# Other places in a hand written order of issue: cosformer attention and a feed-forward layer on one core

## The chip, the cores and the metric

The kernel runs on one core of a Trainium2 chip. The metric is the time of one execution on the device in microseconds (us). A core has engines that run side by side, each with its own queue of instructions in program order: TensorE (PE in the profile; matmuls from SBUF into PSUM), VectorE (DVE), ScalarE (ACT), GpSimd (POOL) and SyncE (SP, which here issues nearly all DMAs). An instruction that waits holds up everything behind it in its engine's queue.

## The reference

Linear attention with a cosine weighting, and then a feed-forward layer over all its tokens. There are 8 batches, 8 heads, 576 positions and 64 features per head; 4608 tokens of 512 features go through 512 to 2048 to 512.

```python
pos = np.arange(S); theta = np.pi / 2 * pos / S
def phi(x):                                  # 64 -> 128 features
    r = np.maximum(x, 0)
    return np.concatenate([r * cos(theta), r * sin(theta)], axis=-1)
q_p, k_p = phi(q), phi(k)
kv  = einsum('bhsf,bhsd->bhfd', k_p, v)
z   = k_p.sum(axis=2)
num = einsum('bhsf,bhfd->bhsd', q_p, kv)
den = einsum('bhsf,bhf->bhs', q_p, z) + 1e-6
x   = (num / den) as [4608, 512]
h   = x @ w_in                               # 512 -> 2048
out = maximum(0.01 * h, h) @ w_out           # 2048 -> 512
```

## The kernel before

**Groups.** The tokens are handled in nine groups. Group g from 0 to 7 holds the first 512 tokens of batch g; group 8 holds the last 64 tokens of all eight batches. A group passes these steps, named by the functions that issue them:

- `loads` (SP): q, k and v of the batch, each 1 MB in float32, into `qst`, `kst`, `vst`; small tails into `ktl`, `vtl`.
- `k_part(b, j, part, engine)` and `q_part(g, j, part, engine)`: relu and cosine (part 0, "c") or sine (part 1, "s") weight for the j-th 128 tokens, float32 to float16, on VectorE (`L240`) or ScalarE (`L238`). Results: `kpm`, `kpt` (the tail, j = 4) and `qp`. `v_part` casts v (`vmain` in two halves, `vtail`).
- `kv_all` (PE): k_p^T v of all heads into `ps_kv`, copied to `kv` on ScalarE.
- `q_transpose_dma(g, j)` (SP): a DMA transpose of `qp` into `qpT`, called qT g j below. It needs both parts of this j.
- `num(g, j)` (PE `L380`): numerator and denominator into the single PSUM buffer `ps_num`; then three VectorE steps, `den` (L391), `rden` (L395) and the product `xs` (L396).
- `x_transpose_dma(g, j)` (SP `L357`): `xs` into `xT`, called xT g j below. Batch 2 has PE transposes in its place (`x_transpose`).
- `x_sums(g, s)`, s = 1 to 4 (DVE `L254`, tiles `xw`, `x`): differences of blocks of `xT`, each needing all four xT.

**The feed-forward layer of groups 2 to 8** takes 2x2 blocks and seven products in place of eight. `p1(g, t, n, bank)` (PE `L785`) is product n = 1 to 7 of a pair t of hidden rows, four matmuls of 256 columns into one of four PSUM banks; `seed`, `lrelu`, `u_copy`, `u_lrelu` (ScalarE, L795, L798, L805, L812) and `u_add` (VectorE L251) combine and apply the leaky ReLU into tile `g`. Product 5 opens the bank JOIN, `u_add(g, t, 1)` reads it, and product 3 then adds into that bank, so product 3 waits for the read. Groups 2 and 3 do four hidden rows (6, 7, 14, 15) with plain matmuls, `f1_one` (PE L495), each followed by its own activation (L770). The second layer has `g_sums` (DVE, L251 and L254, tiles `g`, `gs`), `p2` (PE L890), `o_copy` (ScalarE L908), `o_add` (DVE L251) and `o_store` (SP). `w1_sums` and `w2_sums` are sums of the weights on VectorE.

**The order.** From group 1 on nothing is planned by a scheduler. Each step is entered with `put(position, function, arguments)`, the list is sorted by position, and the functions issue their instructions in that order, so a position is a place in the queue of every engine that the step uses. Between engines only the data dependencies order the work. The positions stand in tables:

- `F1_AT`, `F4_AT`: places of the steps behind p1 (seed, copies, adds, leaky ReLU), relative to the product; F1_AT for groups 2 and 3, F4_AT from group 4.
- `F2_AT`, `F24_AT`: of the copies, adds and stores behind p2.
- `W1_AT`, `W2_AT`, `R_AT`: of the weight sums. `G1_AT` (group 1), `G_AT` (2), `G3_AT` (3), `G4_AT` (4 to 7), `GL_AT` (8): of g_sums.
- `ENG[b]`: which engine does each cast of batch b. `AT[b]`: positions of the casts, loads, transposes, num and x_sums of batch b; entry n of `xs` is x_sums(b, n + 1). Entry 5 of both serves batches 5 to 8.

`top[g]` is the position at which group g's first product stands: 46, 104, 162, then 56 more for each group. The entries of AT[2] and AT[3] are absolute; those of AT[4] and AT[5] are relative to `top[b]`. The order is set by these lines:

```python
put(s0 + at_["qs"][j], q_part, b, j, 1, eng["qs"][j])
put(s0 + at_["qt"][j], q_transpose_dma, b, j)
put(s0 + at_["xs"][j], x_sums, b, j + 1)
...
for _, _, f, args in sorted(line, key=lambda e: e[:2]):
    f(*args)
```

Of the kernel before, what the change touches and what calls it, by code (L numbers as in the profile page):

```python
# [18 lines left out]
def kernel(  # L19
# [798 lines left out]
    F1_AT = {'seed': (0.3, 0.7, 0.5), 'u1': (1.0, 1.0, 1.0), '11': (5.3, 1.3, 2.8), 'u2': (0.3, 0.7, 0.5), '22': (1.8, 0.6, 0.2), '21': (0.5, 0.8, 1.9), '12': (0.5, 1.6, 1.1), 'out': (2.7, 2.7, 2.1)}

    P_AT = (  # L820
# [3 lines left out]
    )  # L824
# [3 lines left out]
    F4_AT = {'seed': 1.0, 'u1': 4.1, '11': 7.9, 'u2': 7.6, '22': 9.4, '21': 10.3, '12': 11.2, 'out': 12.9}

    def f1_stream(g):  # L830

        evs = [(-0.1, quarters, (g,))]
        for t in range(3 if g < ALL else 4):
            if g < ALL:
                at_, a = P_AT[t], (g + t) % 2
            else:
# [90 lines left out]
            )  # L927

    F24_AT = {'u0': 2.7, '11': -0.2, 'u1': 1.7, 'u2': -0.7, '22': 0.6, '21': 0.5, '12': 0.0, 'low': 1.9, 'top': 3.1}
    F2_AT = {'u0': 0.7, '11': -0.7, 'u1': -0.1, 'u2': -0.9, '22': -0.5, '21': -0.1, '12': 0.9, 'low': 2.5, 'top': 3.3}  # L930
# [236 lines left out]
```

## Time and profile before

| | |
|---|---|
| Time, median of 3 runs | 271.64 us (271.63 to 271.68) |
| The profiled execution's own time | 272.37 us |
| Its span in the profile | 270.6 us |
| Granted TensorE clock, mean | 1.00 |
| Instructions | 6617 |
| DMA | 57.05 MB, mean 211 GB/s |
| HBM read, written | 36.70 MB, 9.44 MB |

The profile is of one execution. Its page gives each engine's busy time, the span in 40 slices, the chain of work that ended last, and the costliest groups of instructions. The timeline has a row for each instruction or run of like instructions: start, length, engine, line, operation, output and inputs, and in brackets the idle time before it with the instruction that ended it. The length of a row holds some pipelining, so an engine often starts the next instruction before the length of the last is over; the distance of two starts is then the cost.

### The profile page before, as it was taken

The page shows a single profiled execution, that of the slowest core. Times are in us where ns is not written, and L with a number is a line of the kernel's source. Part 1 is how long each engine was busy: PE and PEld are TensorE (multiplying, and loading weights), DVE is VectorE, ACT ScalarE, POOL GpSimd, SP SyncE. Part 2 cuts the span into 40 slices and gives each one's busy share as a digit, 9 for nine tenths or more (in the row PEclk, how much of TensorE's full clock was granted, in tenths as well). Part 3 has the DMA queues.
Part 4 walks back from the last instruction along what each step waited for, and adds up shares of the span by engine and source line. Part 5 has one row for each costly group of instructions (what it writes and reads, how often), then busy time and mean ns, then how long its engine had stood idle before and what let it go on. Part 6 is the DMA issues. An engine that isn't in the chain of part 4 may idle for free.

```text
span 270.6 us, 6617 instructions
## 1 busy us (share of the span) xinstructions
PE 263.6 (97%) x2668; PEld 226.3 (84%) x2668; DVE 201.9 (75%) x446; ACT 200.6 (74%) x331; POOL 10.5 (4%) x21
## 2 busy tenths in 40 slices
PE   8989999999999999999999999999999999999994
PEld 6875455765898989889999999999999889999984
DVE  5965798797986897889779696978577757644653
ACT  6846556696878998798899789978966757776621
POOL 1057001000000000000000000000000000000000
PEclk9999999999999999999999999999999999999999
DMA  6999999979999969998999699977384312200324
GB/s 211 343 394 409 398 370 373 378 161 285 280 232 340 163 209 226 318 168 226 301 273 138 189 265 273 186 207 155 72 141 153 62 41 97 80 0 2 148 46 119
DMA packets 87150, 57.05 MB, mean 211 GB/s; under 512 B 56656, under 2 KB 82256, under 8 KB 86608
## 3 DMA queue, kind: packets, MB, share of 16 engines
q1 hardware_dynamic: 86672, 56.24, 78.9%
q8 instruction: 21, 0.34, 0.5%
q10 hardware_dynamic: 448, 0.39, 0.4%
q14 instruction: 9, 0.07, 0.1%
HBM read 36.70 MB, written 9.44 MB: 171 GB/s over the span
## 4 chain that ended last, share of the span: by engine, by line
PE 70%; DMA 4%; DVE 2%; ACT 1%; issue 0%; DVEq 0%
PE ps_o L890 31%; PE ps_h L785 27%; PE ps_h L495 3%; DMA qst<-in_q_dram 3%; PE ps_h L890 3%; PE ps_num L380 2%; PE ps_kv L289 2%; DMA xT<-xs 1%; DVE gs L254 0%; PE ps_kv L298 0%; ACT g L798 0%; PE ps_xt L445 0%; DVE xw L254 0%; DVE xs L396 0%; DVE w L254 0%
## 5 line engine op out<-in xcount | busy, mean ns | idle before, releaser
L890 PEld LDWEIGHTS <-g 128*128 128x128 f16 x648 | 62.6, 98 | 7.4 <-DVE g L251 0.3
L251 DVE TENSOR_TENSOR u<-ps_h,u 128x512 f32<-128x512 f32 x52 | 35.8, 688 | 25.5 <-PE ps_h L785 22.2
L890 PE MATMUL ps_o<-w,g 128*128 128x256 f16 x352 | 51.2, 273 | 0.0
L785 PEld LDWEIGHTS <-w 128*128 128x128 f16 x416 | 44.4, 114 | 1.3
L785 PE MATMUL ps_h<-xT,w 128*128 128x256 f16 x288 | 43.3, 273 | 0.0
L812 ACT ACTIVATE g<-u 128x1024 f16<-128x1024 f32 x26 | 27.5, 1058 | 10.9 <-DVE u L251 10.8
L785 PEld LDWEIGHTS <-wa 128*128 128x128 f16 x312 | 34.0, 113 | 1.8 <-DVE xw L254 0.6
L798 ACT ACTIVATE g<-ps_h 128x512 f16<-128x512 f32 x52 | 31.2, 602 | 5.7 <-PE ps_h L785 5.7
L805 ACT COPY u<-ps_h 128x512 f32<-128x512 f32 x52 | 30.4, 584 | 5.4 <-PE ps_h L785 5.4
L890 PE MATMUL ps_o<-wb,g 128*128 128x256 f16 x232 | 33.5, 273 | 0.0
L785 PE MATMUL ps_h<-xw,wa 128*128 128x256 f16 x208 | 31.3, 273 | 0.3 <-DVE xw L254 0.3
L890 PEld LDWEIGHTS <-gs 128*128 128x128 f16 x256 | 24.9, 98 | 3.0
L908 ACT COPY ob<-ps_o 128x512 f32<-128x512 f32 (+1 forms) x32 | 17.9, 561 | 10.0 <-PE ps_o L890 8.5
L495 PE MATMUL ps_h<-xT,w 128*128 128x512 f16 (+1 forms) x104 | 24.7, 363 | 0.0
L396 DVE TENSOR_TENSOR xs<-ps_num,rden 128x512 f16<-128x512 f32 x28 | 19.4, 692 | 1.0
L890 PE MATMUL ps_o<-w,gs 128*128 128x256 f16 x120 | 17.8, 273 | 0.0
L251 DVE TENSOR_TENSOR ob<-ps_o,ob 128x512 f32<-128x512 f32 (+1 forms) x22 | 14.9, 675 | 3.7 <-ACT ob L908 1.4
L890 PE MATMUL ps_o<-wb,gs 128*128 128x256 f16 x120 | 17.5, 273 | 0.0
L254 DVE TENSOR_TENSOR gs<-g 128x1024 f16<-128x1024 f16 x16 | 11.0, 689 | 8.3 <-ACT g L812 8.1
L795 ACT COPY ps_h<-ps_h 128x512 f32<-128x512 f32 x26 | 14.9, 572 | 2.2 <-PE ps_h L785 1.4
L785 PE MATMUL ps_h<-xT,wa 128*128 128x256 f16 x104 | 15.6, 273 | 0.0
L785 PE MATMUL ps_h<-xw,w 128*128 128x256 f16 x104 | 15.6, 273 | 0.0
(113 smaller groups left out, 408.9 us busy)
## 6 DMA issues: line engine op xcount, KB each, us to landing
qst<-in_q_dram SPq DMA_DIRECT2D x7, 1024.0 KB, 7.1
out_dram<-ob SPq DMA_DIRECT2D x14, 512.0 KB, 2.9
kst<-in_k_dram SPq DMA_DIRECT2D x6, 1024.0 KB, 8.3
vst<-in_v_dram SPq DMA_DIRECT2D x6, 1024.0 KB, 7.6
w1st<-in_moe_w_in_dram SPq DMA_DIRECT2D x8, 512.0 KB, 9.8
w2st<-in_moe_w_out_dram SPq DMA_DIRECT2D x4, 1024.0 KB, 12.3
kst<-in_k_dram SPq DMA_DIRECT2D x4, 512.0 KB, 7.1
vst<-in_v_dram SPq DMA_DIRECT2D x4, 512.0 KB, 7.0
```

Source lines behind the costliest of these rows:

```text
L251: nc.vector.tensor_tensor(out=o, in0=a, in1=b, op=ALU.add)
L254: nc.vector.tensor_tensor(out=o, in0=a, in1=b, op=ALU.subtract)
L289: nc.tensor.matmul(ps[:, n * NE : (n + 1) * NE - 1], lhsT=kpm[:, h, j, :], rhs=vmain[:, h, j, 0 : NE - 1], start=(n == 0 and j == 0), stop ...
L396: nc.vector.tensor_tensor(out=xs, in0=ps[:, :, 0 : 4 * NE].rearrange("p a (b e) -> p a b e", e=NE)[:, :, :, 0:D], in1=rden.rearrange("p (a ...
L495: nc.tensor.matmul(ps[:, lo:hi], lhsT=w1[m // 4][c // 2][:, c % 2, m % 4 : 512 : 4], rhs=st["xT", g][:, c, lo:hi], start=(c == 0 and lo == 0),
L785: nc.tensor.matmul(bank[:, p], lhsT=w(c), rhs=st["xb", g][n][:, c], start=(fresh and p == 0 and c == 0), stop=(c == 1), skip_group_check=True,
L795: nc.scalar.copy(bank1[bj], bank1[bi])
L798: nc.scalar.activation(st["g" + nm, g][:, 2 * t : 2 * t + 2], bank1[bi], AF.Lrelu)
L805: nc.scalar.copy(st["u", g, t][:, n], bank1[bi])
L812: nc.scalar.activation(st["gt", g][:, :, 1, 2 * t : 2 * t + 2], st["u", g, t], AF.Lrelu)
L890: nc.tensor.matmul(bank[..., lo:hi], lhsT=st[G2[n], g][:, m, pair * P : (pair + 1) * P], rhs=W2[n](m)[:, lo:hi], start=(fresh and m == 0), ...
L908: nc.scalar.copy(o_at(g, half_, col, pair), bank_of(bi, pair, pair is None))
```

## The change

Only the tables of positions and the table of engines change. No operation, buffer or data type does, and `P_AT` is only written on one line. Of the casts, these change engine: in batch 2, k parts kc[1] (to ScalarE), ks[0] and ks[3] (to VectorE); in batch 3, several; in batch 4, v's tail (to VectorE), qs[2] (to ScalarE) and qs[3] (to VectorE); in batches 5 to 8, kc[3] and qc[3] (to ScalarE), qs[0] and qs[3] (to VectorE). Everything else moves by between a tenth of a position and some twenty within its queue. The tables with their lines:

```diff
-    F1_AT = {'seed': (0.3, 0.7, 0.5), 'u1': (1.0, 1.0, 1.0), '11': (5.3, 1.3, 2.8), 'u2': (0.3, 0.7, 0.5), '22': (1.8, 0.6, 0.2), '21': (0.5, 0.8, 1.9), '12': (0.5, 1.6, 1.1), 'out': (2.7, 2.7, 2.1)}
+    F1_AT = {'seed': (0.3, 0.8, 1.3), 'u1': (1.0, 0.6, 1.0), '11': (5.7, 1.4, 2.8), 'u2': (0.3, 0.7, 0.5), '22': (1.4, 0.6, 0.2), '21': (0.5, 1.0, 2.1), '12': (0.5, 1.6, 0.5), 'out': (2.7, 2.7, 2.1)}
-    F4_AT = {'seed': 1.0, 'u1': 4.1, '11': 7.9, 'u2': 7.6, '22': 9.4, '21': 10.3, '12': 11.2, 'out': 12.9}
+    F4_AT = {'seed': 1.1, 'u1': 3.7, '11': 7.9, 'u2': 7.6, '22': 9.3, '21': 9.1, '12': 11.1, 'out': 12.9}
-    F2_AT = {'u0': 0.7, '11': -0.7, 'u1': -0.1, 'u2': -0.9, '22': -0.5, '21': -0.1, '12': 0.9, 'low': 2.5, 'top': 3.3}
+    F2_AT = {'u0': 1.5, '11': -0.5, 'u1': 0.0, 'u2': -0.9, '22': -0.2, '21': -0.1, '12': 0.5, 'low': 2.7, 'top': 3.3}
-    W1_AT = {3: (38.5, 53.5)}
-    W2_AT = {2: (16.0,), 3: (29.5, 18.5), 4: (75.5,)}
-    G1_AT = {3: (15.0, 31.0), 2: (16.5, 33.5), 1: (25.5, 39.5), 4: (63.0, 45.5)}
-    G_AT = {3: (-6.5, 10.5), 2: (0.0, 11.0), 1: (17.5, 32.5), 4: (23.0, 29.5)}
-    G3_AT = {3: (-3.5, 10.0), 2: (2.0, 23.0), 1: (12.5, 29.5), 4: (26.5, 49.0)}
-    G4_AT = {3: (-6.5, 12.5), 2: (3.0, 17.0), 1: (26.0, 18.0), 4: (33.0, 54.0)}
-    GL_AT = {3: (-15.5, 13.0), 2: (-1.5, 13.5), 1: (5.5, 16.2), 4: (17.5, 32.0)}
-    R_AT = (28.5, 30.0, 46.0, 45.0)
+    W1_AT = {3: (38.5, 51.5)}
+    W2_AT = {2: (16.0,), 3: (29.5, 18.5), 4: (70.0,)}
+    G1_AT = {3: (15.0, 32.5), 2: (26.0, 35.5), 1: (20.5, 34.0), 4: (54.0, 40.5)}
+    G_AT = {3: (-6.5, 10.0), 2: (8.5, 11.0), 1: (17.0, 31.5), 4: (24.0, 34.5)}
+    G3_AT = {3: (-4.0, 10.0), 2: (2.0, 15.0), 1: (13.5, 33.5), 4: (26.5, 54.0)}
+    G4_AT = {3: (-6.5, 13.0), 2: (0.0, 17.0), 1: (26.5, 18.0), 4: (31.0, 52.0)}
+    GL_AT = {3: (-15.5, 13.0), 2: (9.5, 14.0), 1: (3.5, 14.2), 4: (23.5, 30.5)}
+    R_AT = (20.5, 34.0, 54.0, 45.0)
...
     ENG, batch 4:
-    'v': (DVE, DVE, ACT), ... 'qs': (DVE, DVE, DVE, ACT)
+    'v': (DVE, DVE, DVE), ... 'qs': (DVE, DVE, ACT, DVE)
     AT, batch 3:
-    'num': (69.5, 76.0, 83.0, 89.0), 'xt': (89.5, 92.5, 93.0, 100.5), 'xs': (102.5, 106.0, 104.5, 114.0)
+    'num': (69.0, 76.0, 83.0, 89.0), 'xt': (92.5, 91.5, 94.5, 100.5), 'xs': (101.5, 103.5, 112.0, 114.5)
     AT, batch 4 (relative to 162):
-    'v': (-85.0, -40.5, -44.5), 'kv': (-37.5,), 'qc': (-72.5, -67.5, -58.0, -40.0), 'qs': (-66.5, -51.5, -43.5, -39.0), 'qt': (-52.0, -34.5, -33.0, -32.0)
+    'v': (-77.0, -41.0, -42.5), 'kv': (-37.5,), 'qc': (-72.5, -66.5, -53.0, -48.5), 'qs': (-66.5, -52.0, -43.5, -36.5), 'qt': (-52.5, -37.5, -38.0, -33.0)
     AT, batches 5 to 8 (relative to top; 218 for batch 5):
-    'load': (-103.5, -85.5, -75.5), 'kc': (-64.5, -75.0, -78.0, -50.0, -49.0)
-    'qc': (-87.0, -76.0, -45.0, -40.0), 'qs': (-73.5, -75.5, -44.0, -30.5), 'qt': (-55.0, -53.0, -43.5, -25.5)
-    'xt': (-24.5, -17.8, -17.6, -6.9)
+    'load': (-106.0, -87.5, -79.0), 'kc': (-65.0, -77.5, -73.0, -49.5, -54.0)
+    'qc': (-92.0, -76.5, -46.0, -40.0), 'qs': (-71.0, -75.5, -43.5, -27.5), 'qt': (-55.0, -53.0, -42.5, -25.5)
+    'xt': (-24.5, -25.8, -12.6, -7.4)
```

AT[2] (attention of batch 2) and the lines of AT not shown change in the same manner; num(2,0) and num(2,1) keep positions 19.0 and 20.5.

More of the change, by code (lines that the diff above doesn't have):

```diff
@@ L816 @@
     SEED, JOIN, ALL = 2, 3, 4
[L818 to L820 removed]
[3 rows of a table removed]
[L824 removed]
+    F1_AT = {'seed': (0.3, 0.8, 1.3), 'u1': (1.0, 0.6, 1.0), '11': (5.7, 1.4, 2.8), 'u2': (0.3, 0.7, 0.5), '22': (1.4, 0.6, 0.2), '21': (0.5, 1.0, 2.1), '12': (0.5, 1.6, 0.5), 'out': (2.7, 2.7, 2.1)}
+    P_AT = ({1: 0, 6: 3, 2: 5, 7: 6, 5: 8, 4: 9, 3: 11}, {1: 10, 6: 13, 2: 15, 7: 16, 4: 19, 5: 20, 3: 23}, {1: 21, 6: 24, 2: 26, 7: 27, 5: 28, 4: 30, 3: 31})
     ONE_AT = ((4, 7), (12, 14), (17, 18), (22, 25))
     P4_AT = {1: 0, 6: 3, 2: 5, 7: 6, 5: 8, 4: 9, 3: 11}
[L828 removed]
+    F4_AT = {'seed': 1.1, 'u1': 3.7, '11': 7.9, 'u2': 7.6, '22': 9.3, '21': 9.1, '12': 11.1, 'out': 12.9}
     def f1_stream(g):
@@ L1080 @@
-    R_AT = (28.5, 30.0, 46.0, 45.0)
-    ENG = {2: {'kc': (DVE, DVE, DVE, DVE, DVE), 'ks': (ACT, DVE, DVE, ACT, DVE), 'v': (ACT, DVE, ACT), 'qc': (DVE, DVE, DVE, DVE), 'qs': (DVE, DVE, DVE, DVE)}, 3: {'kc': (ACT, ACT, ACT, DVE, DVE), 'ks': (DVE, DVE, ACT, DVE, DVE), 'v': (DVE, ACT, DVE), 'qc': (ACT, DVE, ACT, ACT), 'qs': (DVE, DVE, DVE, ACT)}, 4: {'kc': (ACT, ACT, DVE, ACT, ACT), 'ks': (DVE, ACT, DVE, DVE, DVE), 'v': (DVE, DVE, ACT), 'qc': (DVE, ACT, ACT, DVE), 'qs': (DVE, DVE, DVE, ACT)}, 5: {'kc': (ACT, ACT, DVE, DVE, ACT), 'ks': (DVE, DVE, DVE, DVE, DVE), 'v': (DVE, ACT, ACT), 'qc': (ACT, ACT, DVE, DVE), 'qs': (ACT, ACT, DVE, ACT)}}
@@ L1082 @@
-    AT = {2: {'kc': (-12.0, -0.5, 13.0, 5.5, 13.0), 'ks': (-22.5, -12.5, -17.0, -10.5, 1.0), 'v': (8.0, 11.0, 13.0), 'kv': (16.5,), 'qc': (-8.5, 2.5, 4.5, 9.0), 'qs': (0.0, 4.5, 7.5, 13.0), 'qt': (6.0, 7.0, 8.0, 14.0), 'num': (19.0, 20.5, 24.0, 27.5), 'xt': (24.4, 24.9, 26.9, 30.9), 'xs': (36.0, 50.0, 39.0, 56.0)}, 3: {'load': (20.5, 24.0, 32.0), 'kc': (37.0, 43.0, 48.0, 52.0, 50.5), 'ks': (34.0, 43.5, 58.5, 50.5, 51.0), 'v': (56.0, 57.0, 59.5), 'kv': (62.0,), 'qc': (26.0, 29.0, 31.0, 36.5), 'qs': (31.5, 29.5, 41.0, 41.0), 'qt': (32.5, 34.5, 44.0, 48.0), 'num': (69.5, 76.0, 83.0, 89.0), 'xt': (89.5, 92.5, 93.0, 100.5), 'xs': (102.5, 106.0, 104.5, 114.0)}, 4: {'load': (-76.5, -104.5, -111.0), 'kc': (-80.0, -58.0, -56.0, -70.5, -49.5), 'ks': (-65.5, -54.5, -65.0, -54.5, -54.0), 'v': (-85.0, -40.5, -44.5), 'kv': (-37.5,), 'qc': (-72.5, -67.5, -58.0, -40.0), 'qs': (-66.5, -51.5, -43.5, -39.0), 'qt': (-52.0, -34.5, -33.0, -32.0), 'num': (-34.0, -28.3, -25.1, -16.4), 'xt': (-19.0, -16.8, -12.1, -6.4), 'xs': (-0.5, 0.0, 9.5, 17.0)}, 5: {'load': (-103.5, -85.5, -75.5), 'kc': (-64.5, -75.0, -78.0, -50.0, -49.0), 'ks': (-71.0, -59.0, -72.0, -60.5, -77.0), 'v': (-60.0, -52.0, -60.5), 'kv': (-46.5,), 'qc': (-87.0, -76.0, -45.0, -40.0), 'qs': (-73.5, -75.5, -44.0, -30.5), 'qt': (-55.0, -53.0, -43.5, -25.5), 'num': (-37.0, -32.3, -19.6, -15.9), 'xt': (-24.5, -17.8, -17.6, -6.9), 'xs': (-2.5, -1.5, -1.5, 16.0)}}
@@ new lines @@
+    ENG = {2: {'kc': (DVE, ACT, DVE, DVE, DVE), 'ks': (DVE, DVE, DVE, DVE, DVE), 'v': (ACT, DVE, ACT), 'qc': (DVE, DVE, DVE, DVE), 'qs': (DVE, DVE, DVE, DVE)}, 3: {'kc': (ACT, DVE, DVE, ACT, DVE), 'ks': (DVE, DVE, DVE, DVE, DVE), 'v': (ACT, ACT, DVE), 'qc': (ACT, DVE, ACT, ACT), 'qs': (DVE, DVE, ACT, DVE)}, 4: {'kc': (ACT, ACT, DVE, ACT, ACT), 'ks': (DVE, ACT, DVE, DVE, DVE), 'v': (DVE, DVE, DVE), 'qc': (DVE, ACT, ACT, DVE), 'qs': (DVE, DVE, ACT, DVE)}, 5: {'kc': (ACT, ACT, DVE, ACT, DVE), 'ks': (DVE, DVE, DVE, DVE, DVE), 'v': (DVE, ACT, ACT), 'qc': (ACT, ACT, DVE, ACT), 'qs': (DVE, ACT, ACT, DVE)}}
@@ new lines @@
+    AT = {2: {'kc': (-12.0, -1.5, 11.0, 5.5, 13.0), 'ks': (-25.0, -11.5, -19.0, -9.5, 1.0), 'v': (9.0, 11.0, 11.0), 'kv': (16.5,), 'qc': (-9.5, -3.5, 3.5, 9.0), 'qs': (0.0, 4.5, 6.5, 13.0), 'qt': (2.0, 7.5, 8.5, 14.5), 'num': (19.0, 20.5, 24.0, 27.5), 'xt': (24.9, 24.4, 27.9, 30.9), 'xs': (36.5, 47.0, 43.0, 59.0)}, 3: {'load': (18.5, 25.0, 31.5), 'kc': (45.0, 53.0, 47.0, 52.0, 51.5), 'ks': (46.5, 43.5, 59.5, 55.5, 48.0), 'v': (56.0, 56.5, 59.5), 'kv': (63.0,), 'qc': (28.0, 29.0, 31.0, 40.5), 'qs': (31.5, 30.0, 33.5, 41.0), 'qt': (32.5, 33.5, 49.0, 49.0), 'num': (69.0, 76.0, 83.0, 89.0), 'xt': (92.5, 91.5, 94.5, 100.5), 'xs': (101.5, 103.5, 112.0, 114.5)}, 4: {'load': (-76.5, -110.5, -112.0), 'kc': (-80.0, -59.0, -57.0, -72.5, -50.0), 'ks': (-66.0, -51.5, -65.0, -53.5, -54.0), 'v': (-77.0, -41.0, -42.5), 'kv': (-37.5,), 'qc': (-72.5, -66.5, -53.0, -48.5), 'qs': (-66.5, -52.0, -43.5, -36.5), 'qt': (-52.5, -37.5, -38.0, -33.0), 'num': (-33.5, -28.3, -25.1, -18.4), 'xt': (-21.0, -5.8, -9.6, -6.4), 'xs': (-0.5, -0.5, 9.5, 8.0)}, 5: {'load': (-106.0, -87.5, -79.0), 'kc': (-65.0, -77.5, -73.0, -49.5, -54.0), 'ks': (-71.0, -58.5, -77.0, -60.5, -77.0), 'v': (-59.5, -52.0, -61.0), 'kv': (-46.5,), 'qc': (-92.0, -76.5, -46.0, -40.0), 'qs': (-71.0, -75.5, -43.5, -27.5), 'qt': (-55.0, -53.0, -42.5, -25.5), 'num': (-37.0, -32.3, -19.6, -15.9), 'xt': (-24.5, -25.8, -12.6, -7.4), 'xs': (-2.5, -1.5, -1.5, 16.0)}}
```

3 rows, old and new, of the table P_AT are left out of this document.

## The prediction

> **What bounds the kernel now.** I read the page's busy shares and slices first, then the chain of waits.
>
> ```profile
> PE 263.6 (97%) x2668; PEld 226.3 (84%) x2668; DVE 201.9 (75%) x446; ACT 200.6 (74%) x331; POOL 10.5 (4%) x21
> PE   8989999999999999999999999999999999999994
> PE 70%; DMA 4%; DVE 2%; ACT 1%; issue 0%; DVEq 0%
> ```
>
> TensorE is the bound: 97% busy, nine tenths or more in nearly every slice, and 70% of the chain that ended last. No matmul is added or taken away, so the change can pay only through stalls of TensorE. The PE view of the waits, from the kernel's start, names few; these two fall where groups 2 and 3 are worked on:
>
> ```profile
> PE ps_num L380 <- DVE xs L396: 0.5, 1, 0.5
> PE ps_h L785 <- DVE xw L254: 0.3, 1, 0.3
> ```
>
> The timeline of PE shows both places (start, length, form).
>
> ```profile
> 60.70 0.42 PE L380 MATMUL ps_num<-kv,qpT 128*128 128x65 f16 x8
> 62.44 0.41 PE L380 MATMUL ps_num<-kv,qpT 128*128 128x65 f16 x8 [0.45 <-DVE xs L396]
> ...
> 95.87 0.60 PE L785 MATMUL ps_h<-xT,wa 128*128 128x256 f16 x4
> 96.31 0.60 PE L890 MATMUL ps_o<-w,g 128*128 128x256 f16 x4
> 97.21 0.63 PE L785 MATMUL ps_h<-xw,wa 128*128 128x256 f16 x4 [0.30 <-DVE xw L254]
> ```
>
> A product starts 0.44 us behind the last (95.87 to 96.31), as long as TensorE waits for nothing; between 96.31 and 97.21 there are 0.90, so the second stall costs 0.46. The first costs 0.6 at most: one f1_pair (two products of twice the width, 0.87) and the num (0.25) fill 1.12 of the 1.74 from 60.70. Together 1.1 us, 0.4% of the time: that is all that issue order behind this point can win. The sum below is made against the profiled execution's 272.37 us (span 270.6, 1.8 around it), 0.73 over the median of 271.64; a stall counts the same in both. About 0.2%, 0.54 us, is what a measurement of this kernel can tell from no change.
>
> **The change, part by part.** *The first stall stays.* It is num(2,0), its three DVE steps, then num(2,1) in the same PSUM buffer. Positions 19.0 and 20.5 of these two are as they were. The DVE rows:
>
> ```profile
> 61.17 0.16 DVE L391 TENSOR_SCALAR den<-ps_num 128x8 f32<-128x8 f32 x1
> 61.60 0.69 DVE L396 TENSOR_TENSOR xs<-ps_num,rden 128x512 f16<-128x512 f32 x1
> ```
>
> den starts when num's results are there (60.70 + 0.42), not when VectorE is free. The casts that change engine ahead of it (two k parts come to VectorE, one leaves, a g_sums of 0.69 goes later) alter only its slack. Nothing won: 0.
>
> *The second stall moves.* DVE rows around it:
>
> ```profile
> 94.87 0.68 DVE L251 TENSOR_TENSOR u<-ps_h,u 128x512 f32<-128x512 f32 x1
> 95.47 0.41 DVE L254 TENSOR_TENSOR xw<-xT 128x512 f16<-128x512 f16 x1
> 95.80 0.69 DVE L254 TENSOR_TENSOR gs<-g,gs 128x1024 f16<-128x1024 f16 x1
> 96.40 0.42 DVE L254 TENSOR_TENSOR x<-xT 128x512 f16<-128x512 f16 x1
> 96.74 0.42 DVE L254 TENSOR_TENSOR xw<-xT,xw 128x512 f16<-128x512 f16 x1
> 91.12 3.89 DMA xT<-xs
> ```
>
> TensorE waits at 97.21 for the last sum, x_sums(3,2), 96.74 + 0.42. Ahead of it stand a g_sums (95.80) and x_sums(3,3) (96.40), 0.60 + 0.34 of issue. After, both go behind it (g_sums 104.0 to 112.5, x_sums(3,3) 104.5 to 112.0), so this stall goes. But x_sums(3,1) goes from 102.5 to 101.5, ahead of u_add(2,2,1) at 102.4, the 94.87 row. VectorE takes its queue in order, and x_sums(3,1) cannot start before the last xT transpose has landed: 91.12 + 3.89 = 95.01. So u_add starts at 95.35 or later (95.02 + 0.33) instead of 94.87 and ends at 96.03 or later (+ 0.68). The product at 95.87 adds into the bank that u_add reads, and waits: 0.2 if the transpose lands as before, 0.4 to 0.5 if it comes 0.25 later, which v_main(4,0) makes likely (−85 to −77 puts its 0.60 of VectorE ahead of the xs that this transpose carries). Moved, not removed: −0.46 + 0.2 to 0.5, taken as −0.05 from the later landing.
>
> *Batch 4 and the load of k5.* SP's rows, then the tile view of the three qpT transposes and of the k load (issue times min/median/max in ns, then us to landing):
>
> ```profile
> 98.01 0.37 SPq L93 DMA_DIRECT2D qst<-in_q_dram  x1
> 99.83 0.36 SPq L916 DMA_DIRECT2D out_dram<-ob  x1
> 100.28 6.19 SPq L346 DMA_TRANSPOSE qpT<-qp  x3
> 106.53 1.35 SPq L93 DMA_DIRECT2D kst<-in_k_dram  x1
> L346 SPq DMA_TRANSPOSE qpT<-qp x3: 1231/2062/2628, 100.3 to 105.2; - x3
> DMA to landing us min/median/max: 4.3/6.0/6.2
> DMA to landing us min/median/max: 6.5/6.5/6.5
> ```
>
> Before, SP issues q5's load, a store, then qT4 1, 2, 3, then k5's load at 106.53, which lands at 113.0. After, the order is qT4 2, store, 1, 3, k5 (positions 124.0, 124.35, 124.5, 129.0, 130.5). The first waits for q4's sin part 2, now on ScalarE; the last for sin part 3, which moves from ScalarE to VectorE:
>
> ```profile
> 101.38 0.48 DVE L240 TENSOR_SCALAR qp<-qst,sin_t 128x512 f16<-128x512 f32 x1
> 101.78 0.69 DVE L251 TENSOR_TENSOR g<-g 128x1024 f16<-128x1024 f16 x1
> 103.60 0.71 ACT L238 ACTIVATE qp<-qst,sin_t 128x512 f16<-128x512 f32 x1
> 106.11 0.69 DVE L251 TENSOR_TENSOR u<-ps_h,u 128x512 f32<-128x512 f32 x1 [1.45 <-PE ps_h L785]
> ```
>
> Part 3 was done at 104.3 (103.60 + 0.71). After, it stands last in a full VectorE queue. From x_sums(3,1) at 95.3 to it I count ten instructions of the 0.60 kind (101.78 to 102.38 is one), five x or w sums of 0.335, five casts of 0.40 (101.38 to 101.78), a tail cast of 0.26 and v4's tail, two small ones taken as 0.52: 6.0 + 1.7 + 2.0 + 0.8 = 10.5, so it ends at 105.8. The idle 1.45 ahead of 106.11 is used up by v4's tail (from ScalarE), this part and a w1_sums. So qT4 3 issues at 105.9 at the earliest, against 105.24: 0.6. Before, the two transposes under q5's load took 2.06 and 2.63 to issue, the free one 1.23. After, qT4 2 starts at 102.5 and ends between 103.7 and 105.1, the store takes 0.4 and qT4 1 1.2 to 1.3: free for qT4 3 between 105.3 and 106.8. The k5 load then issues 0.6 to 1.6 later; I take 0.85, as most of the q load has landed by then.
>
> What waits for k5:
>
> ```profile
> 113.03 0.71 ACT L238 ACTIVATE qp<-qst,cos_t 128x512 f16<-128x512 f32 x1
> 114.25 0.71 ACT L238 ACTIVATE kpm<-kst,cos_t 128x512 f16<-128x512 f32 x1
> 114.87 0.58 ACT L798 ACTIVATE g<-ps_h 128x512 f16<-128x512 f32 x1
> 115.65 0.60 PE L495 MATMUL ps_h<-xT,w 128*128 128x512 f16 x2
> 108.77 0.42 PE L380 MATMUL ps_num<-kv,qpT 128*128 128x65 f16 x8
> ```
>
> On ScalarE two q5 parts ran before the k5 part (113.03 to 114.25); after, the k5 part (140.5) is ahead of them (141.5, 142.5), so ScalarE stands until k5 lands, and behind it queue the q5 parts and the leaky ReLU at 114.87, which frees the bank of the matmuls at 115.65. The three casts took 1.84, so this ReLU starts at 114.87 + x for a k5 that is x later, and ends 0.2 before 115.65 + x: a stall of x − 0.2, which is 0.65 for x = 0.85, and 0.4 to 1.4 over the range. The same SP queue makes qT4 1 late: issued at 104.1 to 105.5 instead of 100.28, landing 4.3 later with the load's traffic gone, 108.4 to 109.8, against num(4,1) at 108.77. That is a stall of 0 to 1.0. These do not add: TensorE, once late by one, is late for the next, and the larger counts. I take 0.7 for both.
>
> *Later.* In batch 6, qT6 3 goes behind an xT6 transpose on SP:
>
> ```profile
> 160.89 1.56 SPq L346 DMA_TRANSPOSE qpT<-qp  x1
> 162.56 1.19 SPq L357 DMA_TRANSPOSE xT<-xs  x1
> DMA to landing us min/median/max: 5.8/5.8/5.8
> 167.98 0.42 PE L380 MATMUL ps_num<-kv,qpT 128*128 128x65 f16 x8
> ```
>
> It would land at 166.7 + 1.2 to 1.7, up to 0.4 past 167.98; a TensorE that is 0.65 late hides that. Without that cover it costs 0 to 0.4. In batches 5, 7 and 8 the k3 casts that go to ScalarE and the later g_sums of group 8 lie beside matmuls that ran without a gap, and cost 0; if their cover goes, each is at most one instruction, 0.6.
>
> Sum: 0 − 0.05 + 0.7 + 0 = 0.65 us: 271.64 + 0.65 = 272.3 (profiled 273.0).
>
> **The rivals.** *Moved only (0.22).* The k5 load is no later than 0.3 (qT4 2 issues in 1.23 and VectorE's queue is shorter than counted), the rest as above: −0.05 plus up to 0.3, 271.6 to 271.9. For it: the 10.5 us are a count of 23 instructions at rounded lengths, and 0.3 less would do. Against: the sin part's place behind ten long ones, which wait for TensorE as well where it is late.
>
> *Faster (0.21).* The xT transposes start earlier, three of the four being ahead of where they were, and the last lands by 94.8, so u_add ends in time; the queue on SP drains as before. The second stall is then gone, −0.46: 271.2. It decides at a landing 0.2 earlier than 95.01, from which u_add ends before 95.87. Against it: the xs that the last transpose carries comes later. With part of the first stall too, or places that the profile cannot show, −0.6 to −1.1: 270.6 to 271.0. I give the part beyond 0.2% 0.12.
>
> *Slower by the transposes' data (0.12).* The k5 load's data move only when those of the transposes issued ahead of it have, now two issued in the 2.6 us before it where there was one. It would land later than its issue by as much as a transpose's own issue, 1.2: x = 0.85 + 1.2, a stall of 1.85, 273.4. It decides where k5 takes over 7 us from issue to landing instead of 6.5. The Trainium skill (DMA: Bandwidth & Descriptors, section "Queues, rings and completion order") says that on each DMA engine descriptors are consumed in ring order, though a later one may finish its write first. By that rule this is how it goes. The trace agrees only in part: the transposes issued under q5's load took 6.0 to landing and the one after it 4.3, and no row shows a load behind two transposes.
>
> *Several (0.05).* qT6 3 or another transpose comes late by more than 0.65 and adds 0.3 to 0.6: 272.6 to 272.9.
>
> **How the numbers follow.** The forecast has 0.40; its own range is 272.0 to 272.9 (0.4 to 1.3 over before), and four fifths of it lie past 0.54. Slower by over 0.2%: 0.32 + 0.12 + 0.05 = 0.49. Faster: 0.12. Same: 0.08 of the forecast, 0.22, and 0.09 of the faster case, 0.39. The range 271.0 to 273.4 leaves out the far end of the faster case (about 0.08) and what lies past 273.4 (about 0.07).
>
> **What would show it.** Right: PE has no wait for xw near 97 but one for u of L251 near 95.9, of 0.3 to 0.5; k5's load issues at 107.1 to 108.1 of the profile's time and its kpm on ScalarE starts with the landing; PE stands near 115.7 or at num(4,1). The step at 62.4 is as it was. Wrong: k5's load issues at 106.5 to 106.8 (then the time is the same), or TensorE has no stall at 95.9 (then faster).

## The result, and the profile after

The changed kernel took 275.4 us (median of 6 runs, 274.82 to 277.49), the kernel before 271.66 (6 runs, 271.2 to 273.51): ratio 1.0135, 95% interval 1.0091 to 1.0179. Measured a second time beside the experiments it took 274.88 against 272.32, ratio 1.0088 (1.0058 to 1.0118). So it is 0.9 to 1.4% slower, 2.6 to 3.7 us by the medians, where 0.65 us was forecast. The way was right, the size was not. (The ratios here and below are those recorded with their intervals; the quotient of two medians can differ from them by up to 0.002.)

The page after (span 275.7; this execution took 277.49, the longest of the six): busy time, and the chain that ended last by engine.

```profile
PE 264.9 (96%) x2668; PEld 226.5 (82%) x2668; DVE 202.8 (74%) x450; ACT 198.5 (72%) x327; POOL 10.6 (4%) x21
PE 71%; DMA 17%; ACT 4%; DVE 3%; SPq 3%; issue 1%; DVEq 0%; ACTq 0%
```

TensorE does the same 2668 matmuls. Transfers have gone from 4% to 17% of the chain that ended last, but 17.7 us of that stand in the first 21 us, and the second profile of the changed kernel has 8%, so the share says little about the change. TensorE's waits beyond those of before:

```profile
PE ps_h L495 <- ACT g L798: 1.5, 2, 0.8
PE ps_num L380 <- DMA qpT<-qp: 1.4, 1, 1.4
...
PE ps_o L886 <- DVE g L254: 0.6, 1, 0.6
PE ps_h L785 <- DVE u L251: 0.6, 1, 0.6
```

Their places on the PE timeline:

```profile
91.32 0.59 PE L495 MATMUL ps_h<-xT,w 128*128 128x512 f16 x2 [0.77 <-ACT g L798]
97.98 0.60 PE L785 MATMUL ps_h<-xT,wa 128*128 128x256 f16 x4 [0.60 <-DVE u L251]
111.90 0.43 PE L380 MATMUL ps_num<-kv,qpT 128*128 128x65 f16 x8 [1.36 <-DMA qpT<-qp]
119.70 0.59 PE L495 MATMUL ps_h<-xT,w 128*128 128x512 f16 x2 [0.74 <-ACT g L798]
153.74 0.61 PE L886 MATMUL ps_o<-w,g 128*128 128x256 f16 x4 [0.60 <-DVE g L254]
```

The stalls at u_add (97.98), num(4,1) (111.90) and f1_one (119.70) are where the prediction had put them. Those at 91 and 153.7 were not foreseen. The wait for xw near 97 is gone, as forecast. SP on the stretch of batch 4:

```profile
99.94 0.37 SPq L93 DMA_DIRECT2D qst<-in_q_dram  x1
104.21 1.24 SPq L346 DMA_TRANSPOSE qpT<-qp  x1
105.54 0.53 SPq L912 DMA_DIRECT2D out_dram<-ob  x1
106.16 4.50 SPq L346 DMA_TRANSPOSE qpT<-qp  x2
110.71 0.57 SPq L93 DMA_DIRECT2D kst<-in_k_dram  x1
```

SP stands from 100.3 to 104.2 for q4's sine part 2; then the last two transposes take 4.5 us, where the prediction counted 2.5. ScalarE behind the k5 load:

```profile
117.22 0.72 ACT L238 ACTIVATE kpm<-kst,cos_t 128x512 f16<-128x512 f32 x1 [0.94 <-DMA kst<-in_k_dram]
117.85 0.71 ACT L238 ACTIVATE qp<-qst,cos_t 128x512 f16<-128x512 f32 x1
118.46 0.71 ACT L238 ACTIVATE qp<-qst,sin_t 128x512 f16<-128x512 f32 x1
119.07 0.58 ACT L798 ACTIVATE g<-ps_h 128x512 f16<-128x512 f32 x1
```

The k5 cast stands at the head of ScalarE's queue until the load lands, and the leaky ReLU that frees the bank ends at 119.65, as the matmuls at 119.70 start.

**Stalls, stage by stage.** The matmuls of group 1 start between 0.8 us earlier and 2.3 us later than in the profile before, from one execution to the next, also in the two kernels whose edits all lie far behind them (f4_sums_only and k2_sums_casts in the table, 0.93 and 2.29 later). The times of one kernel spread by as much, 1 to 3 us. So I compare traces by how much later than in the profile before the same matmul starts, and take differences: "start" is a matmul of group 1 at 54.27 us of before, then what is added up to 97.7, from there to 117, and from there to 185. The first two numbers of a row together are TensorE's lateness at 97.7.

| kernel, one profile each | start | to 97.7 | to 117 | to 185 | sum without start |
|---|---|---|---|---|---|
| changed | +0.13 | +1.48 | +2.44 | +1.02 | +4.9 |
| changed, again | −0.66 | −0.38 | +1.75 | +0.86 | +2.2 |
| e1_b2_back | +0.59 | −0.25 | +1.92 | +0.44 | +2.1 |
| e2_b4_back | −0.52 | +0.04 | +0.13 | +0.53 | +0.7 |
| e3_b2_alone | −0.36 | +0.46 | 0.00 | 0.00 | +0.5 |
| e4_gsum_back | +1.38 | −0.36 | +1.52 | +0.73 | +1.9 |
| f1_qt_order | −0.58 | +1.14 | +0.38 | +0.39 | +1.9 |
| f2_k5_place | −0.52 | −0.43 | +1.10 | +0.73 | +1.4 |
| f3_four_back | −0.77 | −0.45 | +0.29 | +0.09 | −0.1 |
| f4_sums_only | +0.93 | −0.31 | +0.26 | 0.00 | −0.1 |
| k1_store_ahead | +0.33 | −0.36 | +1.26 | +0.76 | +1.7 |
| k2_sums_casts | +2.29 | −0.49 | +0.16 | 0.00 | −0.3 |
| k3_sine_back | −0.58 | −0.31 | +1.74 | +1.39 | +2.8 |
| m1_store_behind | +1.26 | −0.09 | +1.05 | +0.72 | +1.7 |

The stretch from 97.7 to 117, batch 4's transposes and the k5 load, is the steady part of the loss: 1.5 to 2.4 us in the changed kernel and wherever nothing on it was altered, against a forecast of 0.7.

### The profile page after: what moved, and what is told of

Its sections match the earlier page's. It is cut to its first block, busy times and chain, and to the rows that moved or that the text cites. A ratio compares the mean times of both kernels' runs of the same rounds, so it can differ in the third digit from the quotient of the medians.

```text
span 275.7 us, 6609 instructions
## 1 busy us (share of the span) xinstructions
PE 264.9 (96%) x2668; PEld 226.5 (82%) x2668; DVE 202.8 (74%) x450; ACT 198.5 (72%) x327; POOL 10.6 (4%) x21
## 4 chain that ended last, share of the span: by engine, by line
PE 71%; DMA 17%; ACT 4%; DVE 3%; SPq 3%; issue 1%; DVEq 0%; ACTq 0%
PE ps_o L886 25%; PE ps_h L785 21%; PE ps_h L495 6%; PE ps_o L475 5%; PE ps_h L459 4%; DMA w1st<-in_moe_w_in_dram 4%; DMA xT<-xs 3%; DMA vst<-in_v_dram 3%; PE ps_h L886 3%; DMA qst<-in_q_dram 3%; DMA kst<-in_k_dram 2%; PE ps_kv L289 2%; PE ps_num L380 2%; DMA vtl<-in_v_dram 2%; SPq L357 1%
## 5 line engine op out<-in xcount | busy, mean ns | idle before, releaser
L785 PEld LDWEIGHTS <-w 128*128 128x128 f16 x416 | 44.5, 114 | 1.5 <-issue 0.2
L495 PEld LDWEIGHTS <-w 128*128 128x128 f16 x104 | 11.0, 113 | 6.1 <-issue 1.8
L238 ACT ACTIVATE kpm<-kst,cos_t 128x512 f16<-128x512 f32 (+1 forms) x22 | 14.1, 655 | 2.5 <-DMA kst<-in_k_dram 2.5
```

The costliest lines, as they stand in the source:

```text
L238: nc.scalar.activation(o, i, AF.Relu, scale=col)
L495: nc.tensor.matmul(ps[:, lo:hi], lhsT=w1[m // 4][c // 2][:, c % 2, m % 4 : 512 : 4], rhs=st["xT", g][:, c, lo:hi], start=(c == 0 and lo == 0),
L785: nc.tensor.matmul(bank[:, p], lhsT=w(c), rhs=st["xb", g][n][:, c], start=(fresh and p == 0 and c == 0), stop=(c == 1), skip_group_check=True,
```

## The experiments

Two theories stood at first. Q: SP's queue starts 0.9 us late with batch 2's casts, and all later landings follow from that. R: each delay is made where it shows, by the tables of batches 3 and 4.

**Batch 2 as before.**

```diff
-    ENG[2], AT[2]   of the changed kernel
+    ENG[2], AT[2]   of the kernel before
```

> Changed kernel with the engines and positions of batch 2 as before. Theory Q (the queue of SP): two more k2 casts ahead of q2's first sine part on VectorE start the first qpT transpose 0.9 us later (55.54 against 54.62), everything behind it on SP is later by that and more (the k4 load 1.5, the last xT3 transpose 1.5), and each stall of TensorE from 90 us on is a landing that came late. Then the first transpose issues at 54.6 again, the k4 load lands near 88.3 as before, the stall of 0.92 ahead of f1_one near 91 and the 0.24 behind it are gone, the one at u_add falls from 0.75 to 0.2 to 0.5: 1.4 to 2 us less than the changed kernel, about 273.3. Theory R (each delay is made locally, by the tables of batches 3 and 4; batch 2's lateness is slack): 0 to 0.4 less, about 274.8.

Measured: 274.69 against 272.06, ratio 1.0091 (1.0058 to 1.0124), hardly less than the changed kernel. The stall at num(4,1) stayed (1.3 of wait), those near 91 and 97 were not there; but they were not there in the second profile of the changed kernel either. Q falls as the main cause.

**Batch 4 as before.**

```diff
-    ENG[4], AT[4]   of the changed kernel
+    ENG[4], AT[4]   of the kernel before
```

> Changed kernel with the engines and positions of batch 4 as before (order of the four qpT transposes, sine part 3 on ScalarE, v4's first half earlier). Theory Q: the stalls up to 98 us (0.92, 0.24, 0.75, less 0.46) stay, those at num(4,1) (1.48) and at f1_one near 119 (0.9) shrink to what the earlier lateness of SP leaves: 1.5 to 2.4 us less than the changed kernel, about 273. Theory R: nearly everything is made here: 2.5 to 3.3 less, 271.7 to 272.3, and the stall near 91 is gone too, since v4 and k4 are loaded as before.

Measured: 273.47, ratio 1.0056 (1.0036 to 1.0077). The time is what Q forecast, about 273, and not R's 271.7 to 272.3. The trace speaks for R's mechanism: the stage to 117 goes from 1.75 or 2.44 to 0.13, where Q let the stalls at num(4,1) and f1_one(3,15) shrink only. So these two are made in batch 4's tables. The profiled execution was the fastest of twelve (272.53), so what else the median still has over before is not seen in it.

**Batch 2 alone, on the kernel before.**

```diff
-    ENG[2], AT[2]   of the kernel before
+    ENG[2], AT[2]   of the changed kernel
```

> Kernel before with only the engines and positions of batch 2 changed. Theory Q: first qpT transpose at 55.5, the loads behind it 0.9 to 1.5 later, k4 lands late enough to hold up the leaky ReLU behind its first cast: a stall of 0.5 to 0.9 ahead of f1_one near 91, and the stall of 0.46 for x_sums near 97 grows: 0.9 to 1.7 us over before, 272.5 to 273.4. Theory R: within 0.2 of before, 271.5 to 271.9.

Measured: 272.51, ratio 1.0021 (1.0002 to 1.0039). The PE timeline has the only new stall at num(2,1), not at a load:

```profile
62.49 0.41 PE L380 MATMUL ps_num<-kv,qpT 128*128 128x65 f16 x8 [0.87 <-DVE xs L396]
```

This wait was 0.45 before. VectorE has one cast more there (two k parts come, one leaves), and it pushes num(2,0)'s three steps. In the whole change a g_sums that leaves that place on VectorE (G1_AT, 16.5 to 26.0) makes up for it: its row is missing there in both profiles of the changed kernel, and the wait is 0.4; no run has these two edits alone. Neither theory had named that cover, and the 0.45 over before lies between their forecasts, 0.9 to 1.7 and at most 0.2.

**One g_sums back.**

```diff
-    G3_AT = {..., 4: (26.5, 54.0)}
+    G3_AT = {..., 4: (26.5, 49.0)}
```

> Changed kernel with one position back: the second half of g_sums(3, 4) at 49.0 instead of 54.0 behind group 4's start, so that it is ahead of the x_sums of group 5 on VectorE instead of behind x_sums(5,1), which waits for the last xT5 transpose. Both theories: the wait of p2 for it at 153.7 us (0.77) goes. If nothing else is late there, 0.7 to 0.8 us less than the changed kernel, about 274.3; if the product behind it is held up by the same transpose (x_sums again), the time stays within 0.2 of the changed kernel's.

Measured: 274.25, ratio 1.0078 (1.0048 to 1.0107). In the changed kernel VectorE's rows are:

```profile
152.26 0.42 DVE L254 TENSOR_TENSOR xw<-xT 128x512 f16<-128x512 f16 x1 [0.89 <-DMA xT<-xs]
152.60 0.48 DVE L240 TENSOR_SCALAR kpm<-kst,sin_t 128x512 f16<-128x512 f32 x1
153.00 0.68 DVE L254 TENSOR_TENSOR g<-g,gs 128x1024 f16<-128x1024 f16 x1
```

The g_sums(3,4) half (153.00) stands behind x_sums(5,1), which waits 0.89 for the last xT5, and p2 at 153.74 waits for it. With the position back this wait is gone; x_sums(5,1) still waits (0.52) but no longer ahead of g_sums. In the nine profiles that have the place it costs 0.4 to 0.8. In this run 0.65 came in at later products, of which the changed kernel's profiles have 0.2 and 0.4, so the time says less than the trace.

**The order of two transposes.** Theory R became Q4: SP stands behind a transpose whose cast is not done.

```diff
-    AT[4]['qt'] = (-52.5, -37.5, -38.0, -33.0)
+    AT[4]['qt'] = (-52.5, -38.0, -37.5, -33.0)
```

> Changed kernel with two positions exchanged: the second transpose of batch 4's q (qT4 1, position 124.0) ahead of the third (qT4 2, 124.5) and of the store at 124.35, on SP. Theory Q4 (SP stands behind a transpose whose cast is not done): in the changed kernel SP stands some 4 us (q5's load issued at 99.9, qT4 2 at 104.2) for q4's sine part 2, with qT4 1, ready since 99, behind it, and the store's data then slow qT4 1 to 5.7 us. With qT4 1 first, it is issued at 100 to 101, num(4,1) does not wait (1.1 to 1.5 gone), qT4 3 and the k5 load issue 2 to 3 us earlier and the stall at f1_one (0.4 to 0.9) falls as well: 1.5 to 2.2 us less than the changed kernel, a ratio to before of about 1.006. Theory C (the casts: sine part 3 on VectorE holds qT4 3 and with it k5): only the wait at num(4,1) goes, k5 is as late as it was and TensorE waits for the leaky ReLU behind its cast, by 0.9 or more: 0 to 1.2 less.

Measured: 273.54, ratio 1.0037 (1.0013 to 1.0061), 1.9 less than the changed kernel's first median and 1.3 less than its second. SP:

```profile
98.90 0.37 SPq L93 DMA_DIRECT2D qst<-in_q_dram  x1
99.37 2.15 SPq L346 DMA_TRANSPOSE qpT<-qp  x1
101.61 0.53 SPq L912 DMA_DIRECT2D out_dram<-ob  x1
103.15 4.53 SPq L346 DMA_TRANSPOSE qpT<-qp  x2
107.73 1.32 SPq L93 DMA_DIRECT2D kst<-in_k_dram  x1
```

The first transpose goes in at 99.37, num(4,1) does not wait, and of the stage to 117 only 0.38 is left, at f1_one. This was Q4's size. The 4.53 us of the last pair are not all issue: the first of the two ended at 105.14, and the second, qT4 3, went in at 106.45, behind q4's sine part 3, which VectorE ended at 106.38. The stalls near 91 and 97 (0.83 and 0.30 net) did show in this profile.

**The k5 cast behind the q5 casts.**

```diff
-    AT[5]['kc'] = (-65.0, -77.5, -73.0, -49.5, -54.0)
+    AT[5]['kc'] = (-65.0, -75.0, -73.0, -49.5, -54.0)
```

> Changed kernel with one position back, for batches 5 to 8: the cosine cast of the second k part at -75.0 instead of -77.5, on ScalarE behind two q5 casts (141.5, 142.5) as before, instead of ahead of them. If the late k5 load stalls TensorE because its cast is ahead on ScalarE: the two q5 casts run in the wait, the leaky ReLU behind is up to 1.2 us earlier, and the stall of 0.4 to 0.9 at f1_one(3,15) goes: 0.4 to 0.9 less than the changed kernel. If the lateness of k5 matters in itself: the next that needs it (VectorE's casts ahead of u_add, then kv of batch 5) stalls TensorE as long, and the time is within 0.2 of the changed kernel.

Measured: 273.88, ratio 1.0066 (1.0045 to 1.0086). f1_one(3,15) does not wait, num(4,1) does (0.9 of wait). So it is the place of the cast on ScalarE that turns the late load into a stall there; no later user of k5 took it over.

**Four places back.** The two above, g_sums at 49.0, and x_sums(3,1) behind u_add:

```diff
-    AT[3]['xs'] = (101.5, 103.5, 112.0, 114.5)
+    AT[3]['xs'] = (102.5, 103.5, 112.0, 114.5)
```

> Changed kernel with four places as before: the order of qT4 1 and 2, the k cast of f2, the half g_sums(3,4) at 49.0, and x_sums(3,1) behind u_add(2,2,1) at 102.5. If the places named so far make the loss, what is left of it is batch 2's part and the start (0.4 to 0.5), less 0.3 to 0.46 from x_sums(3,2): within 0.3 us of before, ratio 0.999 to 1.002. If the loss is spread over the many other places of the tables: a ratio of 1.004 or more is left.

Measured: 272.25 against 272.22, ratio 1.0021 (0.9996 to 1.0046). Of the waits that the view lists for TensorE in this stretch only the one of before is left (a delay of 0.28 at a product near 115.6 is not listed):

```profile
61.66 0.41 PE L380 MATMUL ps_num<-kv,qpT 128*128 128x65 f16 x8 [0.45 <-DVE xs L396]
```

The many other places of the tables cost nothing that the trace shows (sum −0.1), and the interval of the ratio includes 1.

**The sums alone, on the kernel before.**

```diff
-    AT[3]['xs'] = (102.5, 106.0, 104.5, 114.0);  G_AT[2] = (0.0, 11.0)
+    AT[3]['xs'] = (102.5, 103.5, 108.0, 114.0);  G_AT[2] = (8.5, 11.0)
```

> Kernel before with only the sums around the second stall in another order: g_sums(2,2) half 0 at 112.5 instead of 104 and x_sums(3,3) at 108.0 instead of 104.5, so that x_sums(3,2) (103.5) follows x_sums(3,1) at once, with u_add(2,2,1) still ahead. The wait of 0.46 near 97 goes and TensorE is that much earlier from there on: 0.4 to 0.5 us less than before, ratio 0.998 to 0.9985. Against it: a sum that goes later is late for its product (x_sums(3,3) for n = 7 near 99.4): then nothing is won.

Measured: 272.62, ratio 1.0007 (0.9984 to 1.0030): nothing won. PE, then ScalarE:

```profile
97.24 0.60 PE L890 MATMUL ps_o<-w,g 128*128 128x256 f16 x4
97.87 0.60 PE L785 MATMUL ps_h<-xw,wa 128*128 128x256 f16 x4
...
97.22 0.60 ACT L795 COPY ps_h<-ps_h 128x512 f32<-128x512 f32 x1
97.73 0.73 ACT L238 ACTIVATE kpm<-kst,sin_t 128x512 f16<-128x512 f32 x1
98.36 0.59 ACT L798 ACTIVATE g<-ps_h 128x512 f16<-128x512 f32 x1
```

The sum is early, but the product (97.87) now waits 0.2 for the seed (97.22 + 0.60) and the next f1_one (99.00) 0.27 for the leaky ReLU at 98.36. The stall of 0.46 stood on VectorE only for its last 0.27.

**The sums and two casts on ScalarE.**

```diff
 the edit above, and
-    AT[4]['qc'][2] = -58.0;  AT[4]['ks'][1] = -54.5
+    AT[4]['qc'][2] = -57.0;  AT[4]['ks'][1] = -52.0
```

> Kernel before with the order of sums that was tried alone (x_sums(3,2) straight behind x_sums(3,1)) and, on ScalarE, two casts of batch 4 behind what TensorE waits for: the q4 cosine part 2 behind the seed of group 3 (105.0 instead of 104.0) and the k4 sine part 1 behind the leaky ReLU of (2, 21) (110.0 instead of 107.5). If ScalarE's seed and leaky ReLU were the next to be late once VectorE's sum was early (0.19 and 0.27 of wait with the sums alone): both waits go, 0.4 to 0.46 less than before, ratio 0.9985. If the two casts are late for their own users: the gain stays under 0.2.

Measured: 271.64 against 272.32, ratio 0.9987 (0.9958 to 1.0016). The trace has the stall of 0.46 gone and 0.16 given back at a p2 after it. The ratio is the one forecast, but its interval includes 1, so a version better than both kernels is likely by the trace and not shown by the time.

**The store ahead of the transposes.**

```diff
-    F2_AT: 'top': 3.3
+    F2_AT: 'top': 2.0
```

> Changed kernel with the stores of the first half of a group's output for groups 1 and 2 some six and three positions earlier, so that group 1's store is issued on SP in the 4 us in which it stands ahead of qT4 2, instead of between qT4 2 and qT4 1. If the store's place makes part of the loss (its issue of 0.5, and its data ahead of those of qT4 1 and 3): qT4 1 is issued 0.5 earlier and lands 1 to 1.5 earlier, the wait at num(4,1) of 1.0 to 1.5 shrinks to 0 to 0.4, and the k5 load is 0.5 to 1.5 earlier: 1 to 1.8 us less than the changed kernel. If standing behind the cast is all: 0.3 to 0.5 less.

Measured: 274.46, ratio 1.0063 (1.0038 to 1.0087). The wait at num(4,1) is 0.6 instead of 1.4, but f1_one waits 0.4: the stage to 117 is 1.26. The median is 0.4 below the changed kernel's second one, as forecast for "standing behind the cast is all", and short of the 1 to 1.8 of the other forecast.

**The sine part back on ScalarE.**

```diff
-    ENG[4]['qs'] = (DVE, DVE, ACT, DVE);  AT[4]['qs'][3] = -36.5
+    ENG[4]['qs'] = (DVE, DVE, ACT, ACT);  AT[4]['qs'][3] = -39.0
```

> Changed kernel with q4's sine part 3 on ScalarE and at its position as before. The prediction's step: this part's place at the end of a full VectorE queue makes qT4 3 and the k5 load late by 0.6, so the stall at f1_one(3,15) shrinks by 0.4 to 0.6 and the time by as much. Theory Q4: SP is still busy with qT4 1 when the part is done in either place, so the k5 load issues within 0.2 of the changed kernel's relative to TensorE, and the time is the same within 0.3; the part costs ScalarE 0.6 ahead of kv's copy and of the leaky ReLU, which may stall TensorE by up to that.

Measured: 275.38, ratio 1.0098 (1.0067 to 1.0130): no gain. The part was ready at 103.4 and its transpose still went in at 105.5, because SP was busy with qT4 1. So the sine part, which the prediction named for the late k5 load, is not the cause in the changed kernel.

**The changed kernel again.**

> The changed kernel as it is, beside the others on one chip. All theories: 2.5 to 3.7 us over before, ratio 1.009 to 1.014; TensorE waits 1.0 to 1.5 at num(4,1) for the transpose, 0.4 to 0.9 at f1_one near 118, 0.4 to 0.8 at p2 near 152, and in some executions also near 91 and 97.

Measured: the second ratio above. PE's waits beyond those of before:

```profile
PE ps_num L380 <- DMA qpT<-qp: 1.4, 1, 1.4
...
PE ps_o L886 <- DVE g L254: 0.3, 1, 0.3
```

The stalls near 91 and 97 are missing, the one at f1_one is 0.17. SP's rows show once more what the transposes take; below them qT4 3 by itself, and the sine part 3 that it needs:

```profile
101.56 1.23 SPq L346 DMA_TRANSPOSE qpT<-qp  x1
102.88 0.53 SPq L912 DMA_DIRECT2D out_dram<-ob  x1
103.50 4.56 SPq L346 DMA_TRANSPOSE qpT<-qp  x2
108.11 0.57 SPq L93 DMA_DIRECT2D kst<-in_k_dram  x1
...
105.24 2.82 SPq L346 DMA_TRANSPOSE qpT<-qp  x1
104.31 0.48 DVE L240 TENSOR_SCALAR qp<-qst,sin_t 128x512 f16<-128x512 f32 x1
```

**The store behind the k5 load.**

```diff
-    F2_AT: 'top': 3.3
+    F2_AT: 'top': 4.9
```

> Changed kernel with the store of group 1's first half moved behind the k5 load on SP (position 131.4 instead of 124.35; group 2's moves by three positions with it). In the runs so far one of the transposes issued behind this store ended its issue only when the store had landed, within 0.4 us (changed kernel again: issue ends 108.06, store lands 108.37). If the store's landing is what holds SP: qT4 1 and 3 issue in 1.2 to 1.7 each, qT4 1 at 103, landing before num(4,1) needs it (wait 1.0 to 1.5 gone), the k5 load some 1.2 us earlier against TensorE's start, no stall at f1_one near 117: 1.3 to 2 us less than the changed kernel, ratio about 1.003. If three transposes take 5.6 to 6.4 us of SP whatever stands ahead: qT4 1 still lands 5.5 us after its issue, the wait shrinks by the store's own issue of 0.6 alone, and the time by 0.3 to 0.8.

Measured: 274.3 against 271.8, ratio 1.0084 (1.0054 to 1.0115). SP, then PE:

```profile
103.77 4.99 SPq L346 DMA_TRANSPOSE qpT<-qp  x3
108.81 0.57 SPq L93 DMA_DIRECT2D kst<-in_k_dram  x1
...
117.75 0.59 PE L495 MATMUL ps_h<-xT,w 128*128 128x512 f16 x2 [0.77 <-ACT g L798]
```

From the first transpose to the k5 load SP takes 5.0 us instead of 6.5, qT4 1 lands 4.6 after its issue instead of 5.7, and num(4,1) does not wait. So the store did hold SP. But f1_one(3,15) is now 0.93 late by itself: of two late landings in a row only the later counts, and the one at num(4,1) had stood in front of the other. The stage to 117 is 1.05 instead of 1.75 and 2.44, yet the time is not less than the changed kernel's beyond the intervals, and the forecast of 1.003 was missed.

## Why the prediction was wrong

*What held.* The first stall stayed. The wait for x_sums(3,2) went; u_add took its place by 0.76 in the first profile and not at all in the second, so "moved" was right for one execution and "gone" for another, as the landing of the last xT3 falls. The places of the two largest stalls, num(4,1) and f1_one(3,15), were right: undoing batch 4's tables takes both away, and each of the two positions takes its own. Batch 6's qT6 3 cost nothing behind a late TensorE, as said. Even the path to the k5 load held as far as the last transpose. Less TensorE's lateness at 97.7, qT4 2 went in at 102.6 in both profiles (forecast 102.5), the sine part 3 ended at 105.8 in both (forecast 105.8), and qT4 3 went in at 106.3 (forecast 105.9 at the earliest, SP free between 105.3 and 106.8).

*The term that was mis-sized: "I take 0.7 for both", by the step "I take 0.85".* The two stalls measured 1.75 and 2.44 together. The step that failed is the issue of the last transposes. The prediction gave qT4 1 "1.2 to 1.3" and qT4 3 the free transpose's 1.23; they took 1.65 and 2.75 in the first profile, 1.63 and 2.82 in the second. From qT4 2 to the k5 load SP took 6.5 (101.56 to 108.11, and 104.21 to 110.71) instead of the 4.9 from 102.5 to 107.4. So the k5 load issued 2.6 later than before against TensorE (110.71 − 1.61 and 108.11 + 1.04, against 106.53), not 0.85 and not the 1.6 at the end of the range. I had read the long issues of before (2.06 and 2.63) as the work of q5's load, which would be over. In both profiles that load had landed (105.12 and 102.77) before the pair went in, and it still took 4.5. The rows of before show the other reading: the issue of 2.63 ended at 105.08, and the store issued ahead of it landed at 105.20. Moving the store gave 1.5 of the 6.5 back, 0.6 of it the store's own issue, though a wait of 0.7 for the sine part 3 had come in.

*"These do not add; the larger counts" and "a stall of x − 0.2" held.* Here is how late k5's data landed against 112.99 of before, beside how late num(4,1) and then f1_one(3,15) started, all less TensorE's lateness at 97.7:

| kernel | k5's landing | num(4,1) | f1_one(3,15) |
|---|---|---|---|
| changed | 2.59 | 1.52 | 2.44 |
| changed, again | 1.91 | 1.57 | 1.75 |
| f1_qt_order | 0.53 | 0 | 0.38 |
| m1_store_behind | 1.09 | 0 | 0.94 |
| f2_k5_place | 1.66 | 1.02 | 1.04 |

With the k5 cast at the head of ScalarE, f1_one is late by the landing less 0.15, whatever num(4,1) has waited before it; the runs e1, e4, k1 and k3 give the same. With the cast behind the q5 casts (f2) only num(4,1) counts. So the wait at num(4,1) was mis-sized too, because qT4 1 landed 5.7 after its issue and not 4.3, but it lies inside the loss that k5's landing makes. Nor does it make the k5 load late: that load was issued (108.11 and 110.71) before num(4,1) started (109.30 and 111.90), and the last transpose ahead of it before the wait began.

*The sine part 3* was named as the reason for the late load and was not, in the changed kernel: it was done 0.4 us before SP was free for qT4 3 (104.79 against 105.14, 107.43 against 107.81). It is the next limit behind SP's queue: where that was shortened, SP stood for it, from 105.14 to 106.45 in f1 and from 106.35 to 107.06 in m1.

*What the sum put at nothing behind 117.* It measured 1.02 and 0.86. g_sums(3,4) from 49.0 to 54.0 was not priced. It goes behind a step that waits for a transfer, and costs 0.4 to 0.8. And of the fourth k cast (kc[3]), which goes to ScalarE, the prediction says for batches 5, 7 and 8 that it lies "beside matmuls that ran without a gap" and costs 0. Batch 7's kv product waits for it, with 0.23 of delay, in both profiles of the changed kernel and in those of e4_gsum_back and k3_sine_back. The first profile, weight loads of TensorE (PEld):

```profile
183.86 0.46 PEld L289 LDWEIGHTS <-kpm 128*128 128x128 f16 x13 [0.19 <-ACT kpm L238]
```

The same tables send one more sine part of batches 5 to 8, qs[2], to ScalarE, which the list of casts ahead of the prediction leaves out. No run has these casts back alone.

*The rival with the transposes' data* had the right resource, SP and what is queued ahead of the k5 load, and its price for the two, 1.85, is within the 1.75 to 2.44 measured. That is luck, for its mechanism was not seen: k5 landed 5.75 and 6.5 after its issue, no later than before's 6.5 and not past the 7 that it had named, so the load's own data were not held back. The issue was. The Trainium skill's rule (DMA: Bandwidth & Descriptors, section "Queues, rings and completion order") of descriptors consumed in ring order fits the transposes behind the store, whose landing moved from 5.7 to 4.6 us with the store away, but no run shows the rings.

*Open.* Why an issue is held is not shown. With the store landed at 106.02 (k1), the third transpose still took 2.22 us to issue, so the store is not all of it. The stalls near 91 us (0.93 and 0.59, with 0.24 behind them) appear in two of the ten profiles that have batch 2 as changed together with the rest. There the k4 load landed late (90.04 and 88.98) and its cast held the leaky ReLU on ScalarE. SP had issued that load 1.2 to 1.4 later against the start than before, behind a q3 transpose whose issue took 3.7 instead of the second profile's 2.2. So in these executions SP's queue was late already in group 2, as theory Q has it; in m1 it was too (3.8), but the load landed sooner after its issue (7.9 against 9.1 and more) and no stall came of it. Why SP falls behind in some executions was not found, and with it how much of the first median's 3.7 us this makes.

## What to carry to other kernels

On a queue that issues in order, price a moved transfer by everything between its new place and the next load that someone needs, using issue lengths measured with the same neighbours; a transpose or a store put in front of a load costs the load its whole issue. Where two late landings follow each other, work out which one ends last before pricing the removal of the other. Place a cast that waits for a load behind work that does not, and a sum that a product needs ahead of one that waits for a transfer. And before crediting a stall's removal, look at the other engine's last step before that product: here the next limit stood 0.27 us behind.

## What was not expected of the hardware

In twelve of the fifteen profiles the issue of one of batch 4's transposes ended 0.1 to 0.3 us ahead of the landing of the store issued before it: 108.06 against 108.37 in the second profile of the changed kernel, 110.66 against 110.97 in the first, 105.08 against 105.20 before, 109.82 against 109.99 with the g_sums back. In f1 and f3 one ended with the landing of q5's load instead (105.14 against 105.15, 103.62 against 103.62). With the store moved behind the k5 load the last pair took 3.0 instead of 4.5 us, its wait of 0.7 for a cast left out. The start of the same matmul of group 1 moved between 53.5 and 56.6 us over the profiles, also where every edit lies behind it, which is more than most of the edits are worth.
